# Tail-key transposes copied one unit earlier, and identity matmuls in four units of the first pair, in an attention-plus-MoE kernel on one core

## The chip, the core and the metric

The kernel runs on one core of a Trainium2 chip. The metric is device time in microseconds (us), lower is better, as the median of repeated runs. The engines are PE (TensorE), ACT (ScalarE), DVE (VectorE), POOL (GpSimd) and SP, which issues most of the DMAs; each works through its own instructions in order and waits on semaphores for the others.

## The reference

Attention with a learned position bias, and a feed-forward layer on its output, all in fp32:

```
scores = q @ k^T / sqrt(64) + bias[h]         # 4 batches, 8 heads, 576 queries and keys, head size 64
bias   = relu((log1p|i-j| / log1p(max(i,1))) * w1 + b1) @ w2
attn   = softmax(scores) ; out = attn @ v
x      = out as 2304 tokens x 512
g      = s * relu(x @ w_in)^2 + b             # w_in: 512 x 2048
y      = g @ w_out                            # w_out: 2048 x 512
```

## The kernel before, in words

First the bias of all heads is computed and stored in DRAM (until about 48 us). Then comes attention (48 to 260 us), then the feed-forward layer, which is almost only matmuls (260 to 664 us).

Attention goes by **pairs**: one head and two batches, 16 pairs in all, numbered p = 0 to 15. A pair has five **units** t = 0 to 4 (written u in `step`): four units of 128 queries, and a fifth with the last 64 queries of both batches. A running number is n = 5p + t. `step(n)` writes out by hand what each engine gets, in this order:

1. `probs_t(n)`: PE transposes the probabilities of unit n (tile `pr`, 64 columns at a time, L337) into two PSUM tiles `tps`; ACT (L369) and DVE (L371) copy these into the SBUF tile `pt`, half each. PE can write the next unit's transposes only when both copies are done.
2. `scores(n+2)`: PE computes the scores two units ahead (L273, tile `sps`), DVE adds the bias and finds the minimum (L287), ACT takes the exponential (L298) of the first of the unit's two halves here, and of the second in the next `probs_t`.
3. `av(p-1, t)`: PE multiplies the previous pair's probabilities with its values, one block of keys in each unit, into the accumulator tile `xps` (L408 for whole blocks of 128 keys; L411 for the last 64 keys, which has its turn in unit 2 and reads `ptr`).

The queries of unit t and keys 512 to 575 make a narrow rest. Its transposes, done in units 1 and 2 of a pair, find no room in `tps` and go into columns 320 to 511 of the two PSUM banks of `xps`, the accumulator of the pair before (`spare(j)`, with `END` = 320). The accumulator itself uses columns 0 to 319 of these banks. ACT then copies them to the SBUF tile `ptr`: the **tail copy**, L350. It stands at the head of unit 3's `probs_t`, ahead of unit 3's L369. For p = 0 there is no pair before, and `accs[-1]` is a tile of its own in the same place of PSUM.

The semaphores are set by a framework from reads and writes of tiles. `step` also decodes weights of the feed-forward layer between times (`fill`, in units 0 to 2): L448 is its ACT instruction, which stands ahead of the second exponential of the unit in some pairs.

Of the kernel before, what the change touches and what calls it, by code (L numbers as in the profile page):

```python
# [13 lines left out]
AF = mybir.ActivationFunctionType  # L14
# [12 lines left out]
def attention_moe(ctx, tc, q, k, v, w_in, w_out, dist, par, out):  # L27
    nc = tc.nc
# [7 lines left out]
    END = 320  # L36
# [39 lines left out]
    ident = const.tile([128, 128], F32, name="ident")  # L76
# [125 lines left out]
    qs, ks, vals, tts, bts, pts, units, accs = {}, {}, {}, {}, {}, {}, {}, {}  # L202
# [38 lines left out]
    def split_qk(p, which):  # L241
        if p < NP:
            full = (qs, ks)[which][p]
            t = io.tile([128, 2, 640], F32R, tag=f"r{which}", name="qr" if which == 0 else "kr")
            nc.gpsimd.tensor_scalar(t[:, 0], full, 1.0, 1.0, op0=ALU.mult, op1=ALU.mult)
            nc.gpsimd.tensor_tensor(t[:, 1], full, t[:, 0].bitcast(F32), op=ALU.subtract)
            (qs, ks)[which][p] = t
# [8 lines left out]
    def batch(t, y):  # L256
        return 1 - y if t in (2, 3) else y

    def scores(n):
        p, t = divmod(n, 5)  # L260
        qt, kt = qs[p], ks[p]
        c = slice(128 * t, 128 * t + 128)
        xs = range(width(n))
        ps = [ps_s.tile([128, 2, 512], F32, tag="s", name="sps") for _ in xs]
        mms = []
        for hf in range(2):
            for x in xs:
                d = slice(64 * batch(t, x), 64 * batch(t, x) + 64) if t < 4 else slice(0, 128)
                o = hf * HALF + (64 if x == 0 else 0)
                for i, (a, b) in enumerate(((0, 0), (0, 1), (1, 0))):  # L270
                    mms.append((i, hf, x, ps[x][:, hf, 0:HALF], qt[d, a, c], kt[d, b, o:o + HALF]))
        for i, _, _, o, a, b in sorted(mms, key=lambda e: (e[2] if n < 7 else 0, e[1], e[0])):
            nc.tensor.matmul(o, a, b, start=(i == 0), stop=(i == 2))  # L273
        units[n] = (
            tp.tile([128, 2, S], F32, tag="pr", name="pr"),
            sm.tile([128, 2], F32, tag="mn", name="mn"),
            ps,
        )
        if t == 0:
            sums[p] = sm.tile([128, 3, 4], F32, tag="su", name="su")  # L280

    def biased(n, x):
        p, t = divmod(n, 5)
        _, mn, ps = units[n]
        bias = bts[group[p]][:, t, 64 - 64 * x:64 - 64 * x + S] if t < 4 else bes[p]
        tt = tp.tile([128, S], F32, tag="tt", name="tt")
        nc.vector.tensor_tensor_reduce(  # L287
            tt.rearrange("p (a b) -> p a b", a=2), ps[x][:, :, 0:HALF],
            bias.rearrange("p (a b) -> p a b", a=2),
            -1.0 / ROOT, BIG, ALU.add, ALU.min, mn[:, x:x + 1],  # L290
        )
        tts[n, x] = tt

    def expo(n, x):
        p, t = divmod(n, 5)
        pr, mn, _ = units[n]
        col = 4 * batch(t, x) + t if t < 4 else 8
        nc.scalar.activation(  # L298
            pr[:, x], tts.pop((n, x)), AF.Exp, bias=mn[:, x:x + 1], scale=-1.0,
            accum_out=sums[p][:, col // 3, col % 3:col % 3 + 1])  # L300

    def width(n):
        return 2 if n % 5 < 4 else 1
# [4 lines left out]
    def norm(p):  # L308
        su = sm.tile([128, 9], F32, tag="rw", name="ru", bufs=2)
        nc.vector.tensor_scalar(  # L310
            su.rearrange("p (a b) -> p a b", a=3), sums.pop(p)[:, :, 0:3], 1e-9, None, op0=ALU.add)
        nc.vector.reciprocal(su, su)
        rows[p] = su
# [8 lines left out]
    def norm_load(p):  # L322
        rbs[p] = tp.tile([128, S], F32, tag="rb", name="rb", bufs=2)
        for x in range(2):
            nc.sync.dma_start(out=rbs[p][64 * x:64 * x + 64, :], in_=rs_d[p][x:x + 1, :].broadcast_to([D, S]))

    def probs_t(n):
        p, t = divmod(n, 5)
        if p not in pts:
            pts[p] = (ptp.tile([128, 4, 2, S], F32, tag="pt", name="pt"),  # L330
                      ptp.tile([128, S], F32, tag="ptr", name="ptr"))
        pt, ptr = pts[p]
        halves = [slice(64 * r, 64 * r + 64) for r in range(2)]

        def turn(outs, src, start=True):
            for r, d in enumerate(halves):
                nc.tensor.matmul(outs[r], src[d], ident[d, d], is_transpose=True,  # L337
                                 start=start, stop=True, skip_group_check=not start)

        def tail_of(t):  # L340
            return units[5 * p + t][0].rearrange("p x j -> p (x j)")[:, 512:640]

        def spare(j):
            c = END + 64 * j
            return [accs[p - 1][:, r, c:c + 64] for r in range(2)]

        if p == 0 and t == 1:
            accs[-1] = ps_x.tile([128, 2, 512], F32, tag="x", name="xps")
        if t == 3:
            nc.scalar.activation(  # L350
                ptr[:, 0:384].rearrange("p (t r c) -> p t r c", t=3, r=2),
                accs[p - 1][:, :, END:END + 192].rearrange("p r (t c) -> p t r c", t=3), AF.Copy)
        if (n + 1, 1) in tts:
            expo(n + 1, 1)
        pr = units[n][0]
        pss = [ps_t.tile([128, 512], F32, tag="t", name="tps") for _ in range(2)]
        if t < 4:
            for i in range(8):
                kb, x = divmod(i, 2)
                y = batch(t, x)  # L360
                k0 = 64 * y + 128 * kb
                turn([ps[:, 64 * i:64 * i + 64] for ps in pss], pr[:, y, k0:k0 + 128])
            for j in ((), (0, 1), (2,), ())[t]:
                turn(spare(j), tail_of(j), start=(p == 0))
            for r, d in enumerate(halves):
                o = pt[:, :, :, 128 * t + 64 * r:128 * t + 64 * r + 64]
                i = pss[r].rearrange("p (a x b) -> p a x b", a=4, x=2)
                if r == 0:
                    nc.scalar.activation(o, i, AF.Copy)  # L369
                else:  # L370
                    nc.vector.tensor_copy(o, i)  # L371
            return
        for i in range(4):
            turn([ps[:, 64 * i:64 * i + 64] for ps in pss], pr[:, 0, 128 * i:128 * i + 128])
        turn([ps[:, 384:448] for ps in pss], tail_of(3))
        turn([ps[0:64, 256:320] for ps in pss], pr[:, 0, 512:S])
        turn([ps[0:9, 320:384] for ps in pss], rows.pop(p))
        rts[p] = sm.tile([9, 128], F32, tag="rt", name="rt", bufs=1)
        for r, d in enumerate(halves):
            for o, i in ((rts[p][:, d], pss[r][0:9, 320:384]),  # L380
                         (pt[:, :, r, 512:S], pss[r][:, 0:256].rearrange("p (a b) -> p a b", a=4)),
                         (ptr[halves[1 - r], 512:S], pss[r][0:64, 256:320]),
                         (ptr[:, 384 + 64 * r:448 + 64 * r], pss[r][:, 384:448])):
                if r == 0:
                    nc.scalar.activation(o, i, AF.Copy)
                else:
                    nc.vector.tensor_copy(o, i)
# [176 lines left out]
    def ok(n, x):  # L564
        return 0 <= n < LAST and x < width(n)
# [7 lines left out]
    def step(n):  # L573
        p, u = divmod(n, 5)
        m = n + 2
        cur = 0 <= n < LAST
        if cur:
            probs_t(n)
            if u < 2:
                split_qk(p + 1, u)  # L580
        if cur and u == 3:
            norm(p)
        if ok(m, 0):
            scores(m)
            for x in range(width(m)):
                biased(m, x)
            expo(m, 0)
        if p >= 1:
            av(p - 1, u, 0)
            av(p - 1, u, 1)  # L590
            if u < 3:
                fill()
        if n == 0:
            load_be(1)
        if u == 4 and cur:
            norm_store(p)
        if u == 0 and p > 0:
            if n <= LAST:
                norm_load(p - 1)
            if p > 1:  # L600
                store_xt(p - 2)
            if cur:
                load_be(p + 1)
                load_v(p + 1)
                load_q(p + 2)
                load_k(p + 2)
        if cur:
            for e in loads_at.get((p, u), ()):
                load_bias(*e)
# [38 lines left out]
    def fill():  # L648
        next(filler, None)
# [183 lines left out]
```

## Time and profile before

| | |
|---|---|
| median of 3 runs | 666.89 us (666.74 to 669.74) |
| the profiled execution's own time | 666.35 us |
| its span, first to last instruction | 664.3 us |
| PE busy | 652.2 us (98%) |
| DVE busy | 443.7 us (67%) |
| ACT busy | 351.2 us (53%) |
| POOL busy | 175.4 us (26%) |
| share of PE in the chain that ended last | 91% |
| tail copy L350 | 16 times, 463 to 472 ns each |

The span is what the trace shows; 2.05 us of the execution's time lie outside it. An engine counts as busy while an instruction of it runs; a PE that is busy may still wait within a series, since the ends of matmuls are modelled.

### The profile page before, as it was taken

How to read it: one execution, taken by the hardware profiler on the slowest of the kernel's cores; microseconds unless marked ns; L12 is line 12 of the kernel's file. 1: busy time of each engine (PE TensorE's matmuls, PEld its weight loads, DVE VectorE, ACT ScalarE, POOL GpSimd, SP SyncE). 2: the span in 40 equal slices, each digit the busy share in tenths (PEclk: the TensorE clock that was granted, in tenths of full speed). 3: DMA queues.
4: the chain of work that ended last, by engine and by line, in shares of the span. 5: the costliest groups of instructions: out<-in, count | busy, mean ns of one | idle time of the engine just before them, and what ended most of it. 6: DMA issues, size and time to landing. Idle time of an engine off the chain costs nothing.

```text
span 664.3 us, 13923 instructions
## 1 busy us (share of the span) xinstructions
PE 652.2 (98%) x5330; PEld 505.3 (76%) x5330; DVE 443.7 (67%) x905; ACT 351.2 (53%) x735; POOL 175.4 (26%) x190
## 2 busy tenths in 40 slices
PE   8998999999999998999999999999999999999997
PEld 5667776676667675788888888888888888888886
DVE  7987889999899886466754465664565664344244
ACT  6988788788888786444543333332333332222221
POOL 6991345434443320012220022210022210000000
PEclk9998999999999999999999999999999999999999
DMA  4988677586667533696619335227325233323212
GB/s 139 335 252 269 226 256 242 171 255 193 219 196 221 181 123 96 189 333 208 263 63 336 117 118 190 64 91 277 108 95 189 64 120 135 118 94 141 92 63 96
DMA packets 53842, 115.23 MB, mean 173 GB/s; under 512 B 10640, under 2 KB 18320, under 8 KB 53776
## 3 DMA queue, kind: packets, MB, share of 16 engines
q1 hardware_dynamic: 53568, 114.09, 51.4%
q8 instruction: 42, 0.69, 0.4%
q10 hardware_dynamic: 208, 0.26, 0.1%
q14 instruction: 24, 0.20, 0.1%
HBM read 84.18 MB, written 30.14 MB: 172 GB/s over the span
## 4 chain that ended last, share of the span: by engine, by line
PE 91%; ACT 3%; DVE 2%; DMA 2%; issue 1%; ACTq 0%; DVEq 0%; SPq 0%
PE hps L524 30%; PE o L549 29%; PE xps L408 11%; PE sps L273 9%; PE tps L337 6%; PE bps L168 5%; ACT pr L298 2%; DVE tt L287 1%; DMA bt<-bias 1%; DMA bias<-stg 1%; ACT ptr L350 1%; PE xps L411 1%; PE xps L337 0%; DMA pt__127<-in_par_dram 0%; DVE f L135 0%
## 5 line engine op out<-in xcount | busy, mean ns | idle before, releaser
L549 PE MATMUL o<-wh,gt 128*128 128x512 f32 x576 | 190.4, 390 | 0.0
L524 PE MATMUL hps<-x,wh 128*128 128x512 f32 (+1 forms) x640 | 181.7, 369 | 0.0
L528 ACT ACTIVATE r<-hps 128x512 f32<-128x512 f32 (+1 forms) x80 | 44.4, 555 | 212.8 <-PE hps L524 212.8
L529 DVE SCALAR_TENSOR_TENSOR r<-r,sb 128x512 f32<-128x512 f32 (+1 forms) x80 | 55.8, 697 | 143.9 <-ACT r L528 143.8
L524 PEld LDWEIGHTS hps<-x,wh 128*128 128x128 f32 x640 | 116.9, 188 | 22.5 <-issue 1.0
L298 ACT ACTIVATE pr<-tt,mn 128x576 f32<-128x576 f32 x144 | 110.9, 771 | 39.3 <-DVE mn L287 37.4
L549 PEld LDWEIGHTS o<-wh,gt 128*128 128x128 f32 x576 | 108.2, 188 | 22.2
L524 PE MATMUL hps<-x,wl 128*128 128x512 f32 (+1 forms) x320 | 117.9, 368 | 0.0
L549 PE MATMUL o<-wl,gt 128*128 128x512 f32 x288 | 112.4, 390 | 0.0
L287 DVE CUSTOM_DVE_ANT_0 tt<-sps,bt 128x576 f32<-128x576 f32 x128 | 91.3, 751 | 7.1 <-PE sps L273 6.1
L534 DVE SCALAR_TENSOR_TENSOR gt<-r,sb,gt 128x512 fp32r<-128x512 f32 (+1 forms) x80 | 62.6, 783 | 38.3 <-ACT gt L533 38.3
L273 PE MATMUL sps<-kr,qr 64*128 64x288 f32 (+1 forms) x864 | 87.7, 308 | 0.0
L474 POOL TENSOR_TENSOR wl<-full,wh 128x512 fp32r<-128x512 f32 x32 | 43.7, 1366 | 158.5 <-ACT wh L469 138.0
L408 PE MATMUL xps<-pt,vt 128*64 128x256 f32 (+1 forms) x512 | 76.3, 420 | 3.4 <-ACT ptr L350 1.9
L533 ACT ACTIVATE gt<-r,sb 128x512 fp32r<-128x512 f32 (+1 forms) x80 | 54.5, 681 | 45.5 <-DVE r L529 45.4
L337 PEld LDWEIGHTS tps<-ident,pr 64*128 64x128 f32 x1216 | 45.2, 138 | 40.6 <-issue 20.6
L273 PEld LDWEIGHTS sps<-kr,qr 64*128 64x128 f32 (+1 forms) x864 | 70.7, 188 | 1.1
L524 PEld LDWEIGHTS hps<-x,wl 128*128 128x128 f32 x320 | 60.3, 188 | 10.1
L549 PEld LDWEIGHTS o<-wl,gt 128*128 128x128 f32 x288 | 54.2, 188 | 10.6
L450 POOL TENSOR_SCALAR full<-full 128x512 f32<-128x512 f32 x32 | 23.8, 744 | 140.7 <-ACT full L448 140.5
L337 PE MATMUL tps<-ident,pr 64*128 64x64 f32 x1216 | 57.6, 230 | 2.5 <-ACT pt L369 1.2
L408 PEld LDWEIGHTS xps<-pt,vt 128*64 128x64 f32 x512 | 31.4, 137 | 24.7 <-issue 8.2
(66 smaller groups left out, 665.5 us busy)
## 6 DMA issues: line engine op xcount, KB each, us to landing
x<-xs SPq DMA_DIRECT2D x48, 512.0 KB
bias<-stg SPq DMA_DIRECT2D x36, 295.5 KB
raw<-in_moe_w_in_dram SPq DMA_DIRECT2D x16, 512.0 KB
raw<-in_moe_w_out_dram SPq DMA_DIRECT2D x16, 512.0 KB
xs<-x SPq DMA_DIRECT2D x16, 512.0 KB
bt<-bias SPq DMA_DIRECT2D x7, 1152.0 KB
qt<-in_q_dram SPq DMA_DIRECT2D x16, 320.0 KB
kt<-in_k_dram SPq DMA_DIRECT2D x16, 320.0 KB
```

The source lines that it names most:

```text
L273: nc.tensor.matmul(o, a, b, start=(i == 0), stop=(i == 2))
L287: nc.vector.tensor_tensor_reduce(tt.rearrange("p (a b) -> p a b", a=2), ps[x][:, :, 0:HALF], bias.rearrange("p (a b) -> p a b", a=2), -1.0 ...
L298: nc.scalar.activation(pr[:, x], tts.pop((n, x)), AF.Exp, bias=mn[:, x:x + 1], scale=-1.0, accum_out=sums[p][:, col // 3, col % 3:col % 3 ...
L337: nc.tensor.matmul(outs[r], src[d], ident[d, d], is_transpose=True, start=start, stop=True, skip_group_check=not start)
L408: nc.tensor.matmul(o, vt[:, 4 * x + kb, :], pt[:, kb, x, c], start=(i == 0), stop=(i == 4))
L474: nc.gpsimd.tensor_tensor(lo, full, hi.bitcast(F32), op=ALU.subtract)
L524: nc.tensor.matmul(ps[:, 0:n], w[0, g][:, a, fc], xs_t[s, a][:, j, 0:n], start=(i == 0), stop=(i == 3 * KB - 1))
L528: nc.scalar.activation(r, ps[:, 0:n], AF.Relu)
L529: nc.vector.scalar_tensor_tensor(r, r, sb[:, 0:1], r, op0=ALU.mult, op1=ALU.mult)
L533: nc.scalar.activation(hi, r, AF.Identity, bias=sb[:, 1:2])
L534: nc.vector.scalar_tensor_tensor(lo, r, sb[:, 1:2], hi.bitcast(F32), op0=ALU.add, op1=ALU.subtract)
L549: nc.tensor.matmul(o, gt[:, a, tok], w[1, g][:, fo], start=(fo == 0 and j == 0), stop=(fo == 3 and j == 2))
```

## The change

Three edits. The tail copy moves from the head of unit 3's `probs_t` to the end of unit 2's, behind the copy of `pt`, in all 16 pairs. The accumulator stand-in of the first pair is allocated in unit 0, no longer in unit 1. And in the steps n = 1 to 4, the second to fifth unit, PE gets two 128x128 matmuls of the identity with itself behind the scores, written into columns 0 to 127 of the first bank of that stand-in; nobody reads the result.

```diff
-        if p == 0 and t == 1:
+        if p == 0 and t == 0:
             accs[-1] = ps_x.tile([128, 2, 512], F32, tag="x", name="xps")
-        if t == 3:
-            nc.scalar.activation(
-                ptr[:, 0:384].rearrange("p (t r c) -> p t r c", t=3, r=2),
-                accs[p - 1][:, :, END:END + 192].rearrange("p r (t c) -> p t r c", t=3), AF.Copy)
         if (n + 1, 1) in tts:
             expo(n + 1, 1)
...
                 else:
                     nc.vector.tensor_copy(o, i)
+            if t == 2:
+                nc.scalar.activation(
+                    ptr[:, 0:384].rearrange("p (t r c) -> p t r c", t=3, r=2),
+                    accs[p - 1][:, :, END:END + 192].rearrange("p r (t c) -> p t r c", t=3), AF.Copy)
             return
...
             expo(m, 0)
+        if 0 < n < 5:
+            for _ in range(2):
+                nc.tensor.matmul(accs[-1][:, 0, 0:128], ident, ident, start=True, stop=True)
         if p >= 1:
             av(p - 1, u, 0)
```

What this does to ACT, in the units 2 and 3 of the second pair (and alike in all later ones). The tail copy is L350 before and L369 after, and the copy of `pt` is L369 before and L365 after. Before:

```order
L298 ACTIVATE pr,su<-tt,mn 128x576 [waits DVE_49]
L369 ACTIVATE pt<-tps 128x8x64 [waits PE_49]
L298 ACTIVATE pr,su<-tt,mn 128x576 [waits DVE_49]
L350 ACTIVATE ptr<-xps 128x384 [waits PE_49]
L369 ACTIVATE pt<-tps 128x8x64 [waits PE_49]
```

After:

```order
L298 ACTIVATE pr,su<-tt,mn 128x576 [waits DVE_49]
L365 ACTIVATE pt<-tps 128x8x64 [waits PE_49]
L369 ACTIVATE ptr<-xps 128x384 [waits PE_49]
L298 ACTIVATE pr,su<-tt,mn 128x576 [waits DVE_49]
L365 ACTIVATE pt<-tps 128x8x64 [waits PE_49]
```

The tail copy and the exponential of the fifth unit (L298 in the middle) have changed places; nothing else has moved on ACT.

PE in the same place, from the scores of unit 2's step to the value matmuls of unit 3's, before:

```order
L273 MATMUL sps<-kr,qr 128x288 x5
L411 MATMUL xps<-ptr,vt 64x256 x2
L411 MATMUL xps<-ptr,vt 64x320 x2
L337 MATMUL tps<-ident,pr 128x64 [waits Activation_49]
L337 MATMUL tps<-ident,pr 128x64 [waits DVE_49]
L337 MATMUL tps<-ident,pr 128x64 x14
L273 MATMUL sps<-kr,qr 128x288 [waits Pool_49]
L273 MATMUL sps<-kr,qr 128x288 [waits DVE_49]
L273 MATMUL sps<-kr,qr 128x288 [waits Pool_49]
L273 MATMUL sps<-kr,qr 128x288 x9
L408 MATMUL xps<-pt,vt 64x256 [waits Activation_49]
```

After:

```order
L273 MATMUL sps<-kr,qr 128x288 x5
L411 MATMUL xps<-ptr,vt 64x256 [waits Activation_49]
L411 MATMUL xps<-ptr,vt 64x256
L411 MATMUL xps<-ptr,vt 64x320 x2
L337 MATMUL tps<-ident,pr 128x64 [waits PE_49]
L337 MATMUL tps<-ident,pr 128x64 [waits DVE_49]
L337 MATMUL tps<-ident,pr 128x64 x14
L273 MATMUL sps<-kr,qr 128x288 [waits Pool_49]
L273 MATMUL sps<-kr,qr 128x288 [waits DVE_49]
L273 MATMUL sps<-kr,qr 128x288 [waits Pool_49]
L273 MATMUL sps<-kr,qr 128x288 x9
L408 MATMUL xps<-pt,vt 64x256 x2
```

PE's instructions stand in the same order, but the wait for ACT has moved from the first value matmul of unit 3 (L408) to the first of unit 2 (L411), and with it the first transpose of unit 3 no longer waits for ACT itself.

PE in the steps n = 1 and n = 2 of the first pair, after the change:

```order
L273 MATMUL sps<-kr,qr 128x288 x5
L590 MATMUL xps<-ident 128x128 x2
L337 MATMUL tps<-ident,pr 128x64 [waits DVE_49,Activation_49]
L337 MATMUL tps<-ident,pr 128x64 [waits Activation_49]
L337 MATMUL tps<-ident,pr 128x64 x14
L337 MATMUL xps<-ident,pr 128x64 x2
L273 MATMUL sps<-kr,qr 128x288 [waits DVE_49]
L273 MATMUL sps<-kr,qr 128x288 x5
L590 MATMUL xps<-ident 128x128 [waits Activation_49]
L590 MATMUL xps<-ident 128x128
L337 MATMUL tps<-ident,pr 128x64 [waits PE_49]
```

Before, the same rows stand there without the two L590 rows, and the last transpose shown waits for DVE and ACT. The added pair behind the scores of n = 2 waits for ACT; the pairs of n = 1, 3 and 4 wait for nobody.

## Rows read from the trace of the kernel before

**Rows 1.** Busy us from 70 to 260: length, PE, PEld, DVE, ACT, POOL.

```profile
70.00:260.00 190.00, 187.32 (x2552) 129.46 (x2551) 169.40 (x462) 154.83 (x397) 74.52 (x68) 1.00 0.62 197
```

**Rows 2.** Timeline of pair 5, units 1 to 3: start, us, engine, instruction, idle before.

```profile
120.26 1.04 PE L273 MATMUL sps<-kr,qr 64*128 64x288 f32 x12
121.23 1.19 PE L408 MATMUL xps<-pt,vt 128*64 128x256 f32 x8
...
123.03 0.76 ACT L298 ACTIVATE pr<-tt,mn 128x576 f32<-128x576 f32 x1
...
123.79 0.57 ACT L369 ACTIVATE pt<-tps 128x512 f32<-128x512 f32 x1
124.04 0.77 PE L411 MATMUL xps<-ptr,vt 64*64 64x256 f32 x8
...
125.06 0.78 ACT L298 ACTIVATE pr<-tt,mn 128x576 f32<-128x576 f32 x1 [0.70 <-DVE mn L287]
125.26 1.04 PE L273 MATMUL sps<-kr,qr 64*128 64x288 f32 x12
...
125.84 0.47 ACT L350 ACTIVATE ptr<-xps 128x384 f32<-128x384 f32 x1
...
126.21 0.59 ACT L369 ACTIVATE pt<-tps 128x512 f32<-128x512 f32 x1
126.36 0.63 PEld L408 LDWEIGHTS xps<-pt,vt 128*64 128x64 f32 x8 [0.29 <-ACT ptr L350]
```

**Rows 3.** Timeline of pair 3, unit 2, with a decoding instruction (L448) on ACT.

```profile
95.92 0.66 ACT L448 ACTIVATE full<-raw 128x512 f32<-128x512 f32 x1
...
96.94 0.77 PE L411 MATMUL xps<-ptr,vt 64*64 64x256 f32 x8
...
97.25 0.57 ACT L369 ACTIVATE pt<-tps 128x512 f32<-128x512 f32 x1
97.64 0.88 PE L337 MATMUL tps<-ident,pr 64*128 64x64 f32 x15
```

**Rows 4.** Timeline of pair 4, unit 2 and the head of unit 3.

```profile
110.24 0.77 PE L411 MATMUL xps<-ptr,vt 64*64 64x256 f32 x8
...
110.73 0.57 ACT L369 ACTIVATE pt<-tps 128x512 f32<-128x512 f32 x1
111.36 0.71 PE L337 MATMUL tps<-ident,pr 64*128 64x64 f32 x16 [0.34 <-ACT pt L369]
```

**Rows 5.** Waits between 70 and 260 us: us in total, times, longest.

```profile
PEld xps L408 <- issue: 6.9, 42, 0.2
...
PEld xps L408 <- ACT ptr L350: 5.4, 15, 1.0
```

**Rows 6.** Timeline of pair 0, units 2 and 3.

```profile
56.63 0.57 ACT L369 ACTIVATE pt<-tps 128x512 f32<-128x512 f32 x1
...
57.26 0.65 PE L337 MATMUL tps<-ident,pr 64*128 64x64 f32 x14 [0.21 <-ACT pt L369]
...
57.74 0.78 ACT L298 ACTIVATE pr<-tt,mn 128x576 f32<-128x576 f32 x1 [0.53 <-DVE mn L287]
...
58.01 0.69 DVE L371 COPY pt<-tps 128x512 f32<-128x512 f32 x1 [0.30 <-PE tps L337]
```

**Rows 7.** Identity matmuls of the setup, by line: ns min/median/max, first and last start.

```profile
L104 PE MATMUL wps<-ident x16: 421/421/580, 1.4 to 4.7; 128*128 128x128 f32 x16
```

**Rows 8.** Windows 62 to 65.5 us: columns as above, then PEclk.

```profile
62.00:62.50 0.50, 0.22 (x4) 0.23 (x6) 0.42 (x2) 0.50 (x2) 0.00 (x0) 0.64 0.77 232
62.50:65.50 3.00, 3.00 (x31) 2.53 (x31) 1.11 (x2) 1.72 (x5) 0.99 (x2) 0.50 1.01 339
```

**Rows 9.** Timeline of PE, the heads of three units from pair 1's first on.

```profile
62.28 1.01 PE L337 MATMUL tps<-ident,pr 64*128 64x64 f32 x14 [0.81 <-ACT ptr L385]
...
66.31 0.71 PE L337 MATMUL tps<-ident,pr 64*128 64x64 f32 x16
...
69.04 0.46 PE L337 MATMUL tps<-ident,pr 64*128 64x64 f32 x8
```

## The prediction

> **What bounds the kernel now.** I read the page first: PE is busy for 98% of the span, and 91% of the chain that ended last is PE's. The chain in order of time then shows where it is not: only the first pair, from 48 to 62 us, goes to and fro between ACT, DVE and PE. From there to the end, PE leads. The windows say the same of attention behind the first pair: in 190 us PE is busy for 187.3, DVE for 169, ACT for 155 [rows 1]. So a stall of PE that is added or removed between 62 and 260 us goes into the time almost whole, since the feed-forward layer behind it is PE's too, and has nothing to give back. The question for each edit is therefore: when does PE wait, and for whom?
>
> For this I went through the timeline at the places that the change touches, in all 16 pairs, and looked at the order of the changed kernel for the waits. The table of waits shows what the tail copy costs now.
>
> **The moved copy, the loss.** Before, the first value matmul of unit 3 (L408) waits for the tail copy. After the change that wait stands at the first value matmul of unit 2 (L411), and the copy behind the copy of `pt` on ACT. So PE can start L411 only when ACT has done the copy of `pt` and then the tail copy. When is that? In pair 5, ACT is in unit 2's second exponential from 123.03 us and begins the copy of `pt` at 123.79 [rows 2]. An ACT instruction starts about 0.10 us before the one ahead of it ends (L369 starts 0.37 us after the start of L350, which takes 0.47 us) [rows 2], so the tail copy would start 0.57 - 0.10 = 0.47 us later, at 124.26, take 0.47 us, and end at 124.73. PE follows 0.05 us behind (the copy that began at 125.84 ends at 126.31, PE loads at 126.36) [rows 2]. L411 starts at about 124.78 in place of 124.04: a stall of 0.75 us. Put simply: 1.00 us from the start of ACT's copy of `pt`, less what L411 starts after it now, here 0.25 us.
>
> The trace has this distance for 15 pairs (1 to 15; pair 0 has no value matmuls in its units). In ten it is 0.25 to 0.27 us, as in the rows: 10 x 0.75 = 7.5 us. In four (2, 3, 7, 11) a decoding instruction, L448, stands on ACT ahead of the second exponential, and the copy of `pt` begins after L411 has begun: 97.25 against 96.94, a stall of 1.31 us [rows 3]; the four come to 5.1 us. In pair 4, ACT is late because DVE is, 110.73 against 110.24, a stall of 1.49 us [rows 4]. **Sum: 14.1 us.** A stall of PE does not shrink the next one: both ACT's exponentials and L411 follow from the same scores in unit 1, and nothing in between is touched.
>
> Why must L411 wait at all, if it writes columns 0 to 319 and the copy reads 320 to 511? The trace has the same case before the change: L408 writes other columns than L350 reads, and starts 0.05 us after its end [rows 2]. The Trainium skill, page "PSUM — Partial Sum Buffer", section Terms, says that two engines must not be in the same bank and partitions at once, whichever columns they use. By that rule the wait cannot be dropped and the change costs what is counted here; if columns decided, the copy would cost nothing, which is rival B below. The trace agrees with the rule.
>
> **The moved copy, what comes back.** First, the wait in unit 3 is gone. The table of waits has 5.4 us over 15 times for it; the same weight load without such a wait sits idle for 6.9/42 = 0.16 us, which 15 times is 2.5 us. So 2.9 us come back [rows 5]. In pair 5 it is 0.13 us: from scores to value matmuls 1.10 us in unit 3, 0.97 in unit 1 [rows 2]; the larger pieces are in pairs 4, 8 and 15. Second, where PE has waited in L411 it no longer waits for ACT's copy of `pt` in front of unit 3's transposes: 0.4 us in pair 4 [rows 4], and about 0.2 us in each of the four pairs with L448 (15 transposes take 0.88 us there, 16 take 0.71 otherwise) [rows 3, 4]. That is 1.2 us. ACT itself is not held up: in pair 5 it would be through at 124.73, and the fifth unit's exponential begins at 125.06 [rows 2]. **Net: 14.1 - 2.9 - 1.2 = 10.0 us slower.**
>
> **The identity matmuls.** There are eight, and L104 shows two passes for each (16 for 8) [rows 7], so four passes in each step. What does a pass cost? L104 itself has 16 starts in 3.3 us, 0.22 us each [rows 7]; that is the upper bound, 0.9 us for a step. The scores' passes of 288 columns come 12 to 0.97 us, 0.08 us each [rows 2], so 0.3 us is the lower one. Nearest in data type and place are L408's plain fp32 passes: eight of 256 or 320 columns, two at a time, in 1.19 us [rows 2], which makes about 0.13 us for 128 columns. I take 0.5 us for a step.
>
> In steps 1, 3 and 4 they stand where PE waits for ACT anyway, so I count nothing (0.5 us each if that cover were gone). In step 2 the first of them waits for the first pair's tail copy, as the order shows. ACT begins the copy of `pt` at 56.63, so the tail copy ends at 57.57 (ahead of the exponential at 57.74, which is not delayed) and PE starts the identities at 57.62 [rows 6]. Queued behind them are unit 3's transposes, which now start at 57.26 [rows 6] and then start at about 58.15, 0.9 us later (0.7 to 1.3 by the bounds). DVE's copy of them at 58.01 [rows 6], the next scores, and ACT's exponentials after those move with it, so I count **0.9 us slower**.
>
> **The clock.** After 0.81 us without work on PE [rows 9], the granted clock falls to 0.50 (1.2 GHz) from 62 to 65.5 us [rows 8]. The unit that runs then takes 62.28 to 66.31 = 4.03 us, the next one 2.73 us [rows 9]: 1.3 us lost, on PE's path. The identities of step 4 fill half of that idle time, and those of step 3 more ahead of it. I take it that the clock then holds, **1.3 us faster**; the other bound is nothing.
>
> The Trainium skill, page "TensorE: Matmul & The Clock Gate", section "Part 4: PE-mode transpose", says that transposes do not count as work for the clock as matmuls do. By it, plain identity matmuls would hold the clock where the transposes did not; no row here shows it. The sum would be as I take it.
>
> Allocating the stand-in earlier changes no instruction. **Sum:** 666.35 us, the profiled execution's own time, + 10.0 + 0.9 - 1.3 = 675.95 us. That execution lies 0.54 us under the median of the runs, so I forecast 676.5 us for the median.
>
> **Rivals.**
> A (the forecast), 676.5 us; by the bounds of the identities and some scatter in the 14.1 us, 675 to 677.5.
> B, the wait at L411 is not paid. Then only the gains are left: 2.9 us and 1.3 us, less 0.9 us, 663.6 us. It decides as soon as ACT is through with the tail copy before L411's turn, 0.75 us earlier than reckoned, or if columns and not banks decided. Against it: ACT is in an exponential until 123.79 [rows 2] and cannot start sooner, in any of the 15 pairs.
> C, the stall is partly absorbed: DVE and ACT catch up while PE waits, and the next stalls shrink by half. That gives 666.5 + 7 - 4 = about 670 to 671 us. Against it: PE has only 2.7 us idle in 190 [rows 1], so there is little waiting left to save, and the 0.25 us distance is the same in pairs with and without decoding work.
> D, the new idle time lets the clock fall. It fell after 0.81 us [rows 9]; the new pieces are 0.75 us in ten pairs, 1.2 to 1.5 in five. Each fall costs 1.3 us: 678 us for one, 683 for five. Against it: PE has done value matmuls and scores just before, and the longest wait for the tail copy now is 1.0 us [rows 5], in a stretch without a fall.
> E, the identities do not hold the clock: 677.8 us.
>
> **How the numbers follow.** A 0.45, E 0.25, D 0.15, C 0.08, B 0.07. The time is A's, 676.5. The range 672.5 to 681 holds A, E, and D up to three falls; outside are B, C and the rest of D, not quite 0.2. Half a per cent, about what a measurement of this kernel tells from no change, is 3.3 us: faster is B, 0.07; the same is half of C, 0.04; slower is the rest, 0.89.
>
> **What would show it.** In the profile after: a wait of PE's L411 for ACT's tail copy, 15 times, about 14 us in all; none of L408 for it; L411 0.05 us behind the copy in each pair; a pair's length 0.6 us up, 1.1 us in pairs with L448. In the first pair: the identities of step 2 at about 57.6 us, the first L408 about 1 us later; no window with a clock of 0.50 near 62 us. Wrong would be: L411 starting before the copy has ended (B), stalls well under 0.75 us (C), clock windows of 0.50 between 66 and 260 us (D).

## The result, and the profile after

The changed kernel takes 676.11 us (median of 5 runs, 675.92 to 677.84) against 666.74 us before (5 runs, 664.95 to 669.74): 1.0142 times as long, 95% interval 1.0112 to 1.0172. The change costs 9.4 us. The profiled execution of after is the slowest of the five, 677.84 us.

In the new file the tail copy is L369, ACT's copy of `pt` is L365, DVE's is L367 and the identity matmuls are L590; the value matmuls keep L408 and L411. The head of the page of after:

```profile
span 675.9 us, 13950 instructions
PE 653.5 (97%) x5346; PEld 506.8 (75%) x5346; DVE 443.8 (66%) x905; ACT 352.6 (52%) x735; POOL 175.5 (26%) x190
```

PE has a little more to do than before, and the span is 11.6 us longer: PE must wait more. In the windows of after, one stretch of 200 us (columns as in [rows 1]) says how much:

```profile
70.00:270.00 200.00, 186.55 (x2530) 129.41 (x2530) 168.39 (x458) 155.45 (x393) 76.02 (x70) 1.00 0.60 191
```

PE is idle for 13.45 us here, where it was idle for 2.7 us in 190 [rows 1]. No other engine has a larger share of busy time than before, and the clock is 1.00 throughout. The waits of the same stretch of after name the place (us in total, times, longest):

```profile
PEld xps L411 <- ACT ptr L369: 15.8, 15, 1.5
PE xps L411 <- ACT ptr L369: 12.3, 15, 1.3
PEld xps L408 <- issue: 10.4, 56, 1.4
...
DVE rb L414 <- DMA rb<-rs: 1.5, 1, 1.5
```

L411 waits 15 times for the tail copy (its weight load, PEld, and its matmul, PE, each have a row for the same 15 waits), and L408 waits no longer for a copy into `ptr` [rows 5]. In the timeline of after this is pair 3 (with decoding on ACT), pair 4 and pair 5:

```profile
99.17 0.67 ACT L448 ACTIVATE full<-raw 128x512 f32<-128x512 f32 x1
...
100.49 0.59 ACT L365 ACTIVATE pt<-tps 128x512 f32<-128x512 f32 x1
100.97 0.49 ACT L369 ACTIVATE ptr<-xps 128x384 f32<-128x384 f32 x1
101.51 0.77 PE L411 MATMUL xps<-ptr,vt 64*64 64x256 f32 x8 [1.25 <-ACT ptr L369]
...
114.28 0.57 ACT L365 ACTIVATE pt<-tps 128x512 f32<-128x512 f32 x1
114.75 0.47 ACT L369 ACTIVATE ptr<-xps 128x384 f32<-128x384 f32 x1
115.28 0.77 PE L411 MATMUL xps<-ptr,vt 64*64 64x256 f32 x8 [0.67 <-ACT ptr L369]
...
128.00 0.58 ACT L365 ACTIVATE pt<-tps 128x512 f32<-128x512 f32 x1
128.48 0.48 ACT L369 ACTIVATE ptr<-xps 128x384 f32<-128x384 f32 x1
129.01 0.77 PE L411 MATMUL xps<-ptr,vt 64*64 64x256 f32 x8 [0.67 <-ACT ptr L369]
```

From the start of ACT's copy of `pt` to L411 it is now 1.01 us in pair 5, where it was 0.25 [rows 2]; in pair 3 it is 1.02 us, where L411 came 0.31 us ahead of the copy [rows 3]. Each L411 begins about 0.05 us behind the end of the tail copy (115.28 against 114.75 + 0.47). Measured from the start of the last matmul of the scores before it, and less the 0.22 us that this takes in the timeline before, the 15 stalls are 0.74 to 0.75 us in eleven pairs and 1.18, 1.32, 1.30 and 1.31 us in pairs 2, 3, 7 and 11: 13.3 us in all.

How the loss builds up is seen when the start of L411 in each pair is set against before (all from the two timelines; the last row is the first L524 of the feed-forward layer):

| place | before | after | later by |
|---|---|---|---|
| pair 1 | 70.72 | 71.58 | 0.86 |
| pair 2 | 83.83 | 87.21 | 3.38 |
| pair 5 | 124.04 | 129.01 | 4.97 |
| pair 10 | 189.93 | 198.36 | 8.43 |
| pair 15 | 255.18 | 267.69 | 12.51 |
| first L524 | 262.50 | 274.00 | 11.50 |

Pair 1 already holds one stall of 0.75 us, so what comes ahead of it, identities included, has cost next to nothing against the execution before, in which the clock fell there [rows 8]: from the first transposes to the first L408 it is 15.13 us after and 15.15 before. Pair 2 loses 2.5 us at once: its stall of 1.18 us, and about 1.3 more, beside which stands the 1.5 us that DVE's L414 waits for a load, in the table above. From there a regular pair such as 6, 10, 13, 14 or 15 adds 0.7 us, and pairs 3, 7 and 11 add 1.2 to 1.3 us each. At the end 1.0 us comes back: that is the wait of L408 in unit 3 of pair 15, which before had and after has not.

The first pair in the timeline of after:

```profile
50.16 0.28 PE L337 MATMUL tps<-ident,pr 64*128 64x64 f32 x2 [0.48 <-ACT pr L298]
...
55.05 0.71 PE L590 MATMUL xps<-ident 128*128 128x128 f32 x4
55.69 0.71 PE L337 MATMUL tps<-ident,pr 64*128 64x64 f32 x16
...
57.07 0.58 ACT L365 ACTIVATE pt<-tps 128x512 f32<-128x512 f32 x1
57.54 0.47 ACT L369 ACTIVATE ptr<-xps 128x384 f32<-128x384 f32 x1
...
58.07 0.71 PE L590 MATMUL xps<-ident 128*128 128x128 f32 x4 [0.63 <-ACT ptr L369]
58.72 0.71 PE L337 MATMUL tps<-ident,pr 64*128 64x64 f32 x16
...
65.29 1.19 PE L408 MATMUL xps<-pt,vt 128*64 128x256 f32 x8
```

Four passes hold PE for 0.64 us (55.05 to 55.69), 0.16 us each. In step 2 they start 1.00 us behind the start of ACT's copy of `pt`, as reckoned, and the transposes 1.65 us behind it, where it was 0.63 [rows 6]: 1.0 us later. The window in which the clock had fallen before [rows 8] reads in after:

```profile
62.00:65.50 3.50, 3.48 (x46) 2.94 (x46) 2.86 (x9) 3.48 (x12) 0.00 (x0) 1.00 0.99 294
```

The clock is full here. Whether the identities did that, one profile of each kernel can't say.

### The profile page after: what moved, and what is told of

Its sections match the earlier page's. It is cut to its first block, busy times and chain, and to the rows that moved or that the text cites. A ratio compares the mean times of both kernels' runs of the same rounds, so it can differ in the third digit from the quotient of the medians.

```text
span 675.9 us, 13950 instructions
## 1 busy us (share of the span) xinstructions
PE 653.5 (97%) x5346; PEld 506.8 (75%) x5346; DVE 443.8 (66%) x905; ACT 352.6 (52%) x735; POOL 175.5 (26%) x190
## 4 chain that ended last, share of the span: by engine, by line
PE 80%; ACT 6%; DVE 5%; DMA 4%; issue 3%; POOL 0%; SPq 0%; ACTq 0%; DVEq 0%
PE hps L524 29%; PE o L549 29%; PE sps L273 6%; PE xps L408 5%; PE bps L168 5%; PE tps L337 4%; ACT pr L298 3%; DMA bt<-bias 3%; DVE tt L287 2%; PE xps L411 2%; ACT pt L365 1%; DVE pt L367 1%; ACT ptr L369 1%; DMA bias<-stg 1%; DVE rb L415 0%
## 5 line engine op out<-in xcount | busy, mean ns | idle before, releaser
L524 PE MATMUL hps<-x,wh 128*128 128x512 f32 (+1 forms) x640 | 181.6, 368 | 0.0
L298 ACT ACTIVATE pr<-tt,mn 128x576 f32<-128x576 f32 x144 | 110.8, 771 | 44.3 <-DVE mn L287 41.1
L524 PEld LDWEIGHTS hps<-x,wh 128*128 128x128 f32 x640 | 116.8, 188 | 22.6 <-issue 1.0
L524 PE MATMUL hps<-x,wl 128*128 128x512 f32 (+1 forms) x320 | 117.7, 368 | 0.0
L408 PE MATMUL xps<-pt,vt 128*64 128x256 f32 (+1 forms) x512 | 76.0, 418 | 2.2 <-issue 1.2
L337 PEld LDWEIGHTS tps<-ident,pr 64*128 64x128 f32 x1216 | 43.8, 137 | 38.5 <-issue 26.0
L524 PEld LDWEIGHTS hps<-x,wl 128*128 128x128 f32 x320 | 60.3, 188 | 10.0
L367 DVE COPY pt<-tps 128x512 f32<-128x512 f32 x64 | 43.9, 686 | 19.6 <-PE tps L337 18.2
L337 PE MATMUL tps<-ident,pr 64*128 64x64 f32 x1216 | 55.3, 229 | 1.1 <-ACT pr L298 1.0
```

Of the source, the lines that this page charges most:

```text
L298: nc.scalar.activation(pr[:, x], tts.pop((n, x)), AF.Exp, bias=mn[:, x:x + 1], scale=-1.0, accum_out=sums[p][:, col // 3, col % 3:col % 3 ...
L408: nc.tensor.matmul(o, vt[:, 4 * x + kb, :], pt[:, kb, x, c], start=(i == 0), stop=(i == 4))
L524: nc.tensor.matmul(ps[:, 0:n], w[0, g][:, a, fc], xs_t[s, a][:, j, 0:n], start=(i == 0), stop=(i == 3 * KB - 1))
```

## The experiments

Theory 1 is the prediction's: PE pays because L411 writes the bank that the tail copy reads, and the copy stands ahead of it in program order. The rivals: the identity matmuls carry a part of the time, as a cost or by holding the clock (theory 2); or it is ACT, whose order and load in this place delay all that follows, whatever bank is read (theory 3 in the expectations). A load that sometimes arrives late behind the first pair came up on the way (theory 4): DVE's L414, the multiplication behind pair 0, waits for it, and what is gained or lost ahead of it would go into that wait. Unless it is said otherwise, a diff is against the changed kernel, and the time in each case is the median, set against runs of the kernel before on the same chip.

**The copy alone.** The identities are left out.

```diff
-        if 0 < n < 5:
-            for _ in range(2):
-                nc.tensor.matmul(accs[-1][:, 0, 0:128], ident, ident, start=True, stop=True)
```

> The tail copy moved as in the change, without the identity matmuls. Theory 1 (the loss is PE's wait at the value matmuls of unit 2 for the tail copy): 666.7 + 10.0 = about 676.7 us (676 to 678); L411 waits 15 times, 13 us in all, and the clock window of 0.50 near 62 us stays as before, so slightly above the changed kernel. Theory 2 (the identities in the first pair carry the loss): within 1 us of the kernel before.

Measured: 675.72 us against 666.37, ratio 1.0135 [1.0113, 1.0157]. The waits of this run, 70 to 280 us, and its windows across the place of the old clock fall:

```profile
PE xps L411 <- ACT ptr L369: 12.8, 15, 1.3
```

```profile
60.00:66.00 6.00, 5.18 (x76) 4.25 (x77) 4.90 (x16) 5.42 (x16) 1.01 (x2) 1.00 0.97 301
```

The copy alone makes the whole loss, with the same 15 waits, a little under the 676 to 678 us expected. The second row is a miss: without identities, and with the idle time in front of pair 1's first unit still there (0.82 us in this timeline), the clock did not fall.

**The identities alone.** The tail copy is put back to the head of unit 3.

```diff
+        if t == 3:
+            nc.scalar.activation(
...
-            if t == 2:
-                nc.scalar.activation(
```

> The identity matmuls and the earlier allocation alone; the tail copy stays at the head of unit 3. Theory 1: the identities hold the clock and wait for nobody in step 2, so 1.0 to 1.3 us faster than before, about 665.5 us, no window with a clock of 0.50 near 62 us. If they do not hold the clock: 667 us. Theory 2 (they carry the loss): about 676 us.

Measured: 666.43 us (12 runs) against 666.37 (27 runs), ratio 0.9999 [0.9985, 1.0014]. So these identities, none of which waits for a copy here, neither gain nor cost anything that 12 runs can tell from 1 us; 665.5 us were expected if they hold the clock, and 667 if they don't. The clock holds in this profile, as it does without them. Its window of 60 to 66 us, and L411 of pairs 1 and 2 with L414 between them:

```profile
60.00:66.00 6.00, 5.91 (x90) 4.75 (x86) 5.01 (x16) 5.35 (x16) 1.10 (x2) 1.00 0.96 301
```

```profile
69.36 0.77 PE L411 MATMUL xps<-ptr,vt 64*64 64x256 f32 x8
...
76.86 0.42 DVE L414 TENSOR_TENSOR rb<-xps,rb 128x256 f32<-128x256 f32 x1 [1.11 <-DMA rb<-rs]
...
83.49 0.77 PE L411 MATMUL xps<-ptr,vt 64*64 64x256 f32 x8
```

Against the execution before, in which the clock fell, pair 1 comes 1.36 us sooner (70.72 there), but pair 2 only 0.34 us (83.83 there): in between, L414 waits 1.11 us for its load, for which it did not wait before. So even where a fall is avoided, most of the gain can be lost at this load.

**The same ACT work, another source.** The tail copy stays in its place with its size, but reads a tile in SBUF in place of the accumulator's bank, so that the values of the last keys are not those of the reference.

```diff
-                    accs[p - 1][:, :, END:END + 192].rearrange("p r (t c) -> p t r c", t=3), AF.Copy)
+                    pr.rearrange("p x j -> p (x j)")[:, 0:384].rearrange("p (t r c) -> p t r c", t=3, r=2), AF.Copy)
```

> The changed kernel, but the tail copy reads 384 columns of the unit's probabilities from SBUF in place of the transposes in PSUM (so the values of the last keys are not those of the reference). ACT does the same work in the same place, and PE has nothing to wait for. Theory 1: the 13.3 us of waits at L411 go, and the 0.6 us of the identities of step 2: 676.1 - 13.9 = about 662 to 663 us. Theory 3 (the copy's place on ACT delays the copies of pt and the exponentials, and that is the loss): stays at 675 to 676 us.

Measured: 663.67 us against 666.37, ratio 0.9961 [0.9947, 0.9976]. Pair 5 in the timeline of this run:

```profile
121.71 0.57 ACT L365 ACTIVATE pt<-tps 128x512 f32<-128x512 f32 x1
121.98 0.77 PE L411 MATMUL xps<-ptr,vt 64*64 64x256 f32 x8
122.19 0.51 ACT L369 ACTIVATE ptr<-pr 128x384 f32<-128x384 f32 x1
```

ACT does the same two copies one behind the other, and takes about as long (0.51 us for the tail copy). But L411 starts 0.27 us after the copy of `pt` has begun, as before [rows 2], while the tail copy has not even begun. Only the tie between the copy and the accumulator was taken away, and with it 12.1 us went (+9.4 for the change, -2.7 here), close to the 12.3 us of the table of waits. It is somewhat less than expected (662 to 663 us), all the more as the identities of step 2 don't wait in this version either. ACT's order is not the cause; theory 3 is out.

**The tail copy first.** In unit 2 it is written ahead of the copy of `pt` instead of behind it.

```diff
+            if t == 2:
+                nc.scalar.activation(
...
             for r, d in enumerate(halves):
...
-            if t == 2:
-                nc.scalar.activation(
```

> The changed kernel with one swap on ACT: in unit 2 the tail copy stands ahead of the copy of pt, so it ends 0.48 us sooner. Theory 1 (PE's wait for the tail copy is the loss): each of the 15 waits at L411 is 0.48 us shorter (0.27 in the regular pairs, about 0.8 in those with L448), 6.8 us less in all: 676 - 6.8 = about 669 us (668.5 to 670.5). Theory 3 (the loss is ACT's work in that place): as the changed kernel, 675 to 676 us, since ACT does the same.

Measured: 669.45 us against 666.66, ratio 1.0048 [1.003, 1.0066]. The waits of this run from 70 to 280 us, and pair 5 in its timeline:

```profile
PE xps L411 <- ACT ptr L362: 5.1, 15, 0.8
```

```profile
123.73 0.47 ACT L362 ACTIVATE ptr<-xps 128x384 f32<-128x384 f32 x1
...
124.25 0.77 PE L411 MATMUL xps<-ptr,vt 64*64 64x256 f32 x8 [0.20 <-ACT ptr L362]
```

L411 still starts 0.05 us behind the copy. The copy now ends 0.47 us behind the start of ACT's first copy of the unit, where it was 0.96, and the wait is 7.2 us shorter (12.3 to 5.1); the loss shrinks from 9.4 to 2.8 us. So the price follows from when the copy ends.

**The tail copy behind the value matmuls.** No identities; the copy stays in unit 2, but is written after the value matmuls of the pair before and ahead of the next exponential.

```diff
+    def tail_copy(p):
+        nc.scalar.activation(
+            pts[p][1][:, 0:384].rearrange("p (t r c) -> p t r c", t=3, r=2),
+            accs[p - 1][:, :, END:END + 192].rearrange("p r (t c) -> p t r c", t=3), AF.Copy)
...
-            expo(m, 0)
...
             av(p - 1, u, 0)
             av(p - 1, u, 1)
+        if cur and u == 2:
+            tail_copy(p)
+        if ok(m, 0):
+            expo(m, 0)
```

> No identities; the tail copy one unit sooner, but written behind the value matmuls of unit 2 and ahead of the fifth unit's exponential, so that ACT waits for PE and not PE for ACT. Theory 1: no wait at the value matmuls of unit 2 nor of unit 3; the 2.9 us of waits of before are gone, 666.7 - 2.9 = about 664 us (663.5 to 665.5, as the exponential begins 0.2 us later). Theory 3 (any tail copy in unit 2 is dear, because it delays ACT): 670 us or more.

Measured: 664.47 us (12 runs) against 666.37 (27 runs), ratio 0.9974 [0.996, 0.9988]: quicker than both kernels. The waits of this run, 70 to 280 us, and pair 5 (here the copy is L386, the value matmul L412):

```profile
ACT ptr L386 <- PE xps L412: 5.1, 11, 0.5
PEld xps L412 <- issue: 3.0, 16, 0.5
```

```profile
123.58 0.57 ACT L365 ACTIVATE pt<-tps 128x512 f32<-128x512 f32 x1
...
123.84 0.77 PE L412 MATMUL xps<-ptr,vt 64*64 64x256 f32 x8
...
124.65 0.49 ACT L386 ACTIVATE ptr<-xps 128x384 f32<-128x384 f32 x1 [0.50 <-PE xps L412]
125.04 0.77 ACT L298 ACTIVATE pr<-tt,mn 128x576 f32<-128x576 f32 x1
```

The same two instructions use the same accumulator, but now ACT waits for PE. ACT has the time: it waits 0.50 us and begins its next exponential at 125.04. PE waits for no copy, neither here nor in unit 3.

**The same, with the identities.** The diff of the experiment above, and the identities kept.

> The tail copy behind the value matmuls of unit 2, as in the kernel that took 664.5 us, and the identities as in the change. If the identities gain 1.3 us by the clock: 663.2 us. By theory 4: 664.5 us, within 0.4 us, and DVE's L414 waits about 1 us for rb<-rs.

Measured: 664.62 us against 666.66, ratio 0.9965 [0.9952, 0.9977]: the same as without them. The gain by the clock is not there. The time is the one that theory 4 gave, but its reason is missing: the multiplication L414 (L415 in this file) does not wait in this profile.

**The identities without step 2.** One line: three pairs of identity matmuls, none that waits for a copy.

```diff
-        if 0 < n < 5:
+        if n in (1, 3, 4):
```

> The changed kernel without the identity matmuls of step 2 alone, those that wait for the tail copy. By the prediction's term they cost 0.9 us: 675.2 us. By theory 4 (in the first pair PE's time is not what counts, since the multiplication behind pair 0 waits for its row sums' DMA, rb<-rs, and gains and losses ahead of it go into that wait): the same as the changed kernel, within 0.4 us, with a longer wait for that DMA.

Measured: 675.0 us against 666.66, ratio 1.0124 [1.0108, 1.0139]. The prediction's term of 0.9 us gave 675.2. The changed kernel did not run on this chip; the repeats below set the two side by side. L414 does not wait in this profile, so theory 4's longer wait did not come.

**The loads of weights later.** The version behind the value matmuls, without identities, and two early loads of weights moved behind pair 3's loads of keys, so that less is queued ahead of the load that L414 waits for.

```diff
+                if p == 1:
+                    load_w(*early[0])
+                    load_w(*early[1])
...
-             (store_late, TAIL - 1), (load_q, 2), (load_k, 2), (load_bias, 2, 0, 4), (load_v, 1), (load_w, *early[0]), (load_w, *early[1])),
+             (store_late, TAIL - 1), (load_q, 2), (load_k, 2), (load_bias, 2, 0, 4), (load_v, 1)),
```

> The tail copy behind the value matmuls of unit 2, no identities, and the two loads of 512 KB of weights that SP issues at about 63 us issued later, behind the loads of step 5 (about 75 us; they are first used at about 82 us). Theory 4: rb<-rs lands sooner, DVE's wait for it (1.4 us in the profile of the kernel with the early loads) goes, and with it about 1 us: 663.4 us. If the wait for rb<-rs was not on the path: 664.5 us.

Measured: 664.16 us against 666.66, ratio 0.9958 [0.9945, 0.9971], the lowest median of the three versions with the copy behind the value matmuls. L414 (L415 in this file) does not wait in this profile. But the interval overlaps those of the two versions before it, and L414 does not wait in the profile with identities either, where the loads were not moved. Whether these loads are the cause stays open.

**The tail copy twice.**

```diff
-                nc.scalar.activation(
+                for _ in range(2):
+                    nc.scalar.activation(
```

> The changed kernel with the tail copy done twice in unit 2 (the second writes the same values). Theory 1: each wait at L411 grows by the length of a copy, 0.38 to 0.47 us, 15 times: 5.7 to 7 us more, about 682.5 us (681.5 to 684). Theory 3 (ACT's work in that place is the loss, in proportion): also slower, but the wait of L411 would not grow by the whole copy.

Measured: 687.46 us against 666.66, ratio 1.0307 [1.0286, 1.0328], above what was expected. The waits of this run from 70 to 280 us, pair 3 in its timeline, and the windows behind it (here the copies are L370, the value matmul L412):

```profile
PE xps L412 <- ACT ptr L370: 20.2, 15, 1.8
```

```profile
100.70 0.99 ACT L370 ACTIVATE ptr<-xps 128x384 f32<-128x384 f32 x2
101.75 0.77 PE L412 MATMUL xps<-ptr,vt 64*64 64x256 f32 x8 [1.76 <-ACT ptr L370]
```

```profile
102.00:108.00 6.00, 6.00 (x70) 3.76 (x62) 3.13 (x11) 3.40 (x11) 4.43 (x4) 0.72 0.11 39
...
160.00:166.00 6.00, 5.21 (x58) 3.62 (x60) 2.97 (x8) 3.02 (x8) 3.06 (x4) 0.72 0.32 113
```

The second copy adds 7.9 us to the waits (12.3 to 20.2), 0.53 us in each pair. The rest is the clock: behind two of the four stalls of 1.76 us, in pairs 3 and 7, the mean clock of 6 us is 0.72, so by estimate 0.28 x 6 = 1.7 us of full speed is lost twice, 3.4 us. Together 11.3 us; the two medians on this chip are 687.46 - 676.35 = 11.1 us apart. All four executions show a mean clock of 0.991 to 0.996. Rival D's mechanism exists, then, but it came with stalls of up to 1.8 us, and in no profile with the 0.75 to 1.3 us of the change.

**Three repeats on one chip,** for the cost of the identities: the changed kernel, the copy alone, and the identities without step 2.

> The changed kernel again, beside the two below on one chip: about 676 us. By the profiles so far the first pair takes 15.1 us from its first transposes to the first value matmuls with all identities, 14.6 without those of step 2, 14.1 without any.

> The moved copy without the identities, again. If what the identities take in the first pair (1.0 us in the profiles) goes into the time: 675 us, 1.0 us under the changed kernel beside it. If it is given back behind the first pair, or by a clock that holds: the same as the changed kernel.

> The changed kernel without the identities of step 2, again. If what they take (0.5 us in the profiles) goes into the time: 0.5 us under the changed kernel beside it and 0.5 us over the moved copy alone; if not, equal to both.

Measured: 676.35 us, ratio 1.0145 [1.013, 1.016]; 675.65 us, 1.0135 [1.012, 1.015]; 675.57 us, 1.014 [1.0121, 1.0159]. The first comparison repeats to 0.3 us. All identities together come to 0.7 us here and those of step 2 alone to 0.8 us, in the direction that was predicted, but the intervals overlap. From the first transposes to the first L408 it is 15.13 and 15.53 us in the two profiles of the changed kernel, 14.57 and 14.31 without step 2, 14.06 and 14.40 in the copy alone. So the identities of step 2 cost 0.6 to 1.2 us there; for the other three pairs the two sets of profiles give 0.5 and -0.1 us, so no cost is shown. What the identities cost in the time is about 1 us or less, and not settled.

The stall of pair 4, 0.74 us in the profile of after, is larger in two of these profiles: 1.29 us in that of the copy alone (below) and 1.08 us in the repeat of the changed kernel, with ACT waiting 1.18 and 0.96 us for DVE ahead of it, where it is 0.63 us in after.

```profile
110.96 0.78 ACT L298 ACTIVATE pr<-tt,mn 128x576 f32<-128x576 f32 x1 [1.18 <-DVE mn L287]
...
113.49 0.77 PE L411 MATMUL xps<-ptr,vt 64*64 64x256 f32 x8 [1.22 <-ACT ptr L369]
```

## Why the prediction was right, step by step

- **The wait at L411** (+14.1 us): right, in place and mechanism. 15 waits, 0.05 us behind the copy, 13.3 us. In the four pairs with decoding it came to 5.11 us (predicted 5.1), in the regular ones to 0.75. The difference is pair 4: ACT was late there in the execution before [rows 4] but not in that of after, and the stall was 0.74 us in place of 1.49. ACT was late there again in the copy alone and in the repeat of the changed kernel (1.29 and 1.08 us), and not in the other three profiles with the copy in this place, the repeat of the copy alone and both without step 2. So it comes and goes between executions, and was priced as if it came always.
- **Bank, not columns:** columns did not decide, as forecast: L411 writes other columns than the copy reads, and waits 15 times of 15, while a copy from elsewhere runs under it. By the rule of the Trainium skill that the prediction cites ("PSUM — Partial Sum Buffer", Terms), two engines keep out of one bank; the traces agree: L411 starts 0.05 us behind the end of the copy, and behind the value matmuls the copy starts 0.04 us after L412's end (124.65 against 123.84 + 0.77). But these waits are semaphores that stand in the program, set from reads and writes of tiles, and copy and matmul use the same tile. That the bank decides and not the tile is shown by no run: it would take two tiles in one bank.
- **What comes back** (-2.9 and -1.2 us): right. The waits of L408 are gone from the table: from the scores to the value matmuls of unit 3 the 14 pairs 1 to 14 take 13.5 us in all after and 15.9 before, and pair 15 gives back 1.0 us at its end. From L411 to unit 3's scores they take 17.1 us after and 18.1 before, 1.05 us less. The versions that pay no wait at L411 are 1.9 to 2.7 us quicker than before. For the copy alone the sum of the prediction was 10.0 us; the two comparisons measured 9.35 and 8.99.
- **The identities of step 2** (+0.9 us): the mechanism is right (they start where reckoned, and the transposes come 1.0 us later), a pass takes 0.16 us and not 0.13. In the profiles, those of step 2 cost 0.6 and 1.2 us; in the medians on one chip 0.8 us, inside the intervals. That the others cost nothing is contradicted by neither: -0.1 and 0.5 us in the profiles.
- **The clock** (-1.3 us): this term failed. The fall to 0.50 [rows 8] was an event of the one execution that was profiled, and not a trait of the kernel. The copy alone has the same idle time and no identities, and its clock held; in none of the other profiles, with identities or without, did it fall in this place. A fall like that of [rows 8], some 3.3 us at half speed in an execution of 664 us, takes about 0.0025 off its mean clock. In 34 of 44 later executions of the kernel before, the mean is 0.999 or 1.000, so they had no such fall; their median is 666.41 us. In the other 10 it is 0.997 or less, with a median of 666.74. Where the clock fell in those isn't seen: in the repeat of the copy alone, with a mean of 0.997, it fell in the setup (0.50 from 8 to 11 us) and nowhere in attention. So there was next to nothing to be gained in most executions, and of what there was against the one with the fall, 1.0 of 1.36 us was lost again by L411 of pair 2. The identities alone measured no gain. By the page "TensorE: Matmul & The Clock Gate" of the Trainium skill, Part 4, transposes don't count as work for the clock as matmuls do; no run here shows that plain matmuls made the difference.
- **The total:** 676.5 us forecast, 676.11 measured. In part this is luck: 1.3 us of gain that did not come stand against 0.8 us of stalls that did not come either; what is left is smaller than the runs differ among themselves. The 0.54 us that the forecast adds for the median comes from three runs; later medians of before are 666.37 to 666.74 us, against 666.89.
- **The rivals:** B, no wait, is what the version with another source shows, 663.67 us. That this meets the 663.6 worked out for B is luck: B's sum has the clock term, which failed, and 0.9 us for identities that don't wait in that version. B's condition was not met in the changed kernel. C, absorption, did not occur: the stalls stayed 0.74 to 0.75 us up to pair 15. (C's own sum, 666.5 + 7 - 4, is 669.5 us, not 670 to 671.) D did not occur in the changed kernel's profiles, but did with the copy twice. E is right that the identities bring no gain by the clock, though not because the clock falls in spite of them: it was full with them and without. Its 677.8 us is too high, since it leaves in a fall that is not there in most executions.

## What to carry to other kernels

When a copy and matmuls use one accumulator tile in PSUM, program order decides who waits. One copy of 0.47 us, in the same step of the loop, cost 9.4 us ahead of the matmuls and behind ACT's other copy, 2.8 us as the first of the two, and gained 1.9 us behind the matmuls, because there the engine with spare time waits. A wait that is moved ahead is priced by the distance between the waiter's turn and its releaser's end, pair by pair in the trace. What a single profiled execution shows once (a clock fall, one late pair) is looked for in other executions before it goes into a sum.

## What the runs showed of the hardware

The mean clock differs between executions of one program: 0.994 to 1.000 in 44 of the kernel before. A fall in attention stands behind 0.81 us of idle time in the one profile before [rows 9], none behind 0.82 us at the same place in the copy alone, and none behind 15 stalls of up to 1.3 us in after. With stalls of up to 1.8 us the mean clock was 0.991 to 0.996 in all four executions, and in the profiled one the falls stand behind two of the four longest.

Behind the first pair, DVE's L414 waits for a load for between nothing and 1.5 us: 1.5 in the profile of after, 0.9 in the copy alone, 1.1 in the identities alone, 1.4 in the copy behind the value matmuls, none in the profile before. PE's row is longer by about as much: less the stall of pair 2, L411 of pair 2 comes 14.4, 13.8, 14.1 and 14.5 us behind that of pair 1 in these four, and 13.0 to 13.4 us behind it in the eight profiles without the wait. In after, 1.3 us are lost here at once, in the slowest of five executions, 677.84 against 675.92 to 676.37. Single executions therefore differ by more than the identities cost. Why the load is sometimes late is not settled.
